# A fused attention and feed-forward kernel on one core: earlier cast, fourth tile partly interleaved, W1 pieces regrouped, last tile stored in three pieces

## Chip, cores, metric

One core of a Trainium2 chip. The metric is the device time of one execution in microseconds (us). Each kernel was run 4 to 6 times, on the same chip together with the kernel before. Engines: PE is TensorE, PEld its weight loads, DVE is VectorE, ACT is ScalarE, POOL is GpSimd, SP is SyncE. A bank is one of the kernel's PSUM tiles, in which matmuls are summed; an eviction is the copy out of it by ACT or DVE. The eight heads are handled in two head groups (hg 0 and 1), each with its own part of the transposed softmax, aT, and of W1.

## The reference

```python
B, H, S, Ns, D = 8, 8, 512, 32, 64
# attention of x over a small state, and of the state over x
scores = x @ state.T / 8 ; a  = softmax(scores)  ; xread = a @ state
scores2 = state @ x.T / 8; a2 = softmax(scores2) ; sread = a2 @ x
t = concat([xread, sread], axis=2)      # to tokens x 512
h = t @ w_in                            # 512 -> 2048
out = (h * sigmoid(h)) @ w_out          # 2048 -> 512
```

The kernel never forms xread. For each batch b it makes `W1 = state @ w_in` (per head), and then `h = a @ W1`. "G1" below is that product (two matmuls of 512 columns for each of 16 slices ft of 128 hidden columns), followed by one silu on ACT. "G2" is the product with w_out: four token tiles tt, each summed over the 16 slices, so 64 matmuls a batch. Tokens of sread are a ninth, smaller group at the end.

## The kernel before

The first batches are special. Nothing is resident yet, so batch 0 makes its W1 in pieces between its matmuls. Three token tiles of batch 0 are summed slice by slice; the fourth (tt = 3) is kept back, to give PE work while ACT, DVE and POOL do the softmax of batch 1. I call that stretch, from the scores of batch 1 to its first G1, the handover.

```python
# start of batch 0 (cut)
for u in range(2): copy(nc.vector, <slots of the state>, ps0[...])   # state placement
cast_x(0, nc.vector, 0, 2, 0, 4); cast_x(0, nc.scalar, 2, 2, 0, 4)
...
pe_transpose_x(0, 1, 2, new_h, (nc.vector, nc.scalar))
norm(0, 0); scores(0, 1, 2); exps(0, 1)
norm(0, 1, ((nc.vector, 0, 4),), 2)
w1_cols(0, [(0, 256)], (nc.scalar, nc.scalar))
...
pe_transpose_a(0, 0, nc.vector); pe_transpose_a(0, 1, nc.vector)
g1_half(0, 0); g1_half(1, 0)

# batch 0 (cut)
banks[:] = ["a1", "a2", "a3"]
W0 = {0: (256, 256), 2: (512, 512), 6: (1024, 512), 10: (1536, 512)}
for ft in range(NFT):
    upto(min(ft + LEAD0[ft], ready))                 # G1 and silu up to there
    if ft in W0: w1_cols(0, [W0[ft]], both)          # W1 of batch 0
    if ft in (5, 9, 11): w1_chunks(1, ({5: 0, 9: 1, 11: 2}[ft],), both)   # W1 of batch 1
    ...
    if ft < 14:
        for tt in range(3): G2(0, tt, ft)
...
# handover to batch 1 (cut)
scores(1, 0); scores(1, 1); exps(1, 0); exps(1, 1)
store(0, 2, nc.scalar)
nc.scalar.activation(warm[:], busy[:, 0:1], func=SILU, bias=0.0)   # table load
store(0, 1, nc.vector)
norm(1, 0); norm(1, 1, ((nc.gpsimd, 0, 2), (nc.vector, 2, 2)))
for ft in range(NFT):
    if ft == 5:  w1_chunks(1, (3,), (nc.scalar, nc.scalar))
    if ft == 11: pe_transpose_a(1, 0, nc.scalar); pe_transpose_a(1, 1, nc.vector)
    if ft >= 14: upto(NFT + ft - 12)
    G2(0, 3, ft)

# the last tile: two halves of 256 columns, each evicted by two engines (cut)
def last_half(b, tt, half):
    ...
    for i, eng in enumerate((nc.vector, nc.scalar)):
        copy(eng, o[:, ds(DM // 4 * i, DM // 4)], ps[:, ds(DM // 4 * i, DM // 4)])
    nc.sync.dma_start(out_sread[ds(512, 32), ds(4 * tt, 4), cols], o[:])
```

The softmax here doesn't subtract the row's maximum and nothing guards it: scores larger than these inputs give would overflow.

Of the kernel before, what the change touches and what calls it, by code (L numbers as in the profile page):

```python
# [8 lines left out]
FP32 = mybir.dt.float32  # L9
BF16 = mybir.dt.bfloat16  # L10
# [8 lines left out]
B = 8  # L19
H = 8  # L20
S = 512
NS = 32
D = 64
DM = 512
# [17 lines left out]
def kernel(  # L42
# [141 lines left out]
    make_identity(nc, ident)  # L184
    ones_beside_x(0, nc.gpsimd)
    load_w_in(0, 256)
    load_w_out(0, 2)
    load_w_in(256, 256)
    load_w_out(2, 2)
# [4 lines left out]
    load_w_in(512)  # L194
    load_w_out(4, 4)

    def load_states():
# [44 lines left out]
    def pe_transpose_x(b, hg, nb=2, new=bank, engs=(nc.vector, nc.scalar), only=None):  # L242
# [3 lines left out]
        for u in range(nb) if only is None else only:  # L246
# [8 lines left out]
            copy(engs[u], xT[b][:, ds(m * u, m), ds(2 * hg, 2), :], ps[:])  # L255

    for u in range(2):
        copy(
            nc.vector,
            slots_of(0)[u].rearrange("p g (k n) -> p g k n", n=NS)[:, :, 0:3:2, :],  # L260
            ps0[ds(64 * u, 64)].rearrange("p (g k) m v -> p g k (m v)", g=2),
        )
    cast_x(0, nc.vector, 0, 2, 0, 4)
    cast_x(0, nc.scalar, 2, 2, 0, 4)
    o_tags = ["o0", "o1"]
# [32 lines left out]

    def scores(b, hg, m=4):
        sc_ps[hg] = []  # L300
        for c in range(4):
            if c % m == 0:
                sc_ps[hg].append(bank([128, m, 4, NS], FP32, "ps_sc"))
            for j in range(2):
                nc.tensor.matmul(
                    sc_ps[hg][-1][:, c % m, ds(2 * j, 2), :],
                    xT[b][:, c, 2 * hg + j, :],
                    stT[:, b, 2 * hg + j, :, :],
                    start=True,
                    stop=True,  # L310
                    skip_group_check=True,
                )
# [81 lines left out]

    def pe_transpose_a(b, hg, eng, other=None):
        ps = bank([128, 4, 128], BF16, "ps_at")
        for c in range(4):
            nc.tensor.transpose(ps[:, c, :], an[b, hg][:, c, :, :], ident[:])  # L398
        if other is None:
            copy(eng, aT[b][:, hg, :, :], ps[:])  # L400
        else:
            copy(eng, aT[b][:, hg, 0:2, :], ps[:, 0:2])
            copy(other, aT[b][:, hg, 2:4, :], ps[:, 2:4])

# [49 lines left out]

    def w1_mms(b, cols):
        pss = {}
        if b not in W1:
            W1[b] = wpool.tile([128, 2, DF], BF16, tag="W1", name="W1")
        for f, n in cols:
            for hg in range(2):  # L460
                pss[f, hg] = bank([128, 512], FP32, "ps_w1")
            for s in range(4):
# [13 lines left out]

    def w1_out(b, cols, engs, pss):
        for f, n in cols:
            for hg in range(2):
                copy(engs[hg], W1[b][:, hg, ds(f, n)], pss[f, hg][:, 0:n])  # L480

    def w1_cols(b, cols, engs):
        w1_out(b, cols, engs, w1_mms(b, cols))

# [9 lines left out]

    def g1_half(k, hg):
        b, ft = divmod(k, NFT)
        if hg == 0:
            h_ps[k] = psH.tile([128, 512], FP32, tag="h1", name="h1")
        nc.tensor.matmul(  # L499
            h_ps[k][:],  # L500
            W1[b][:, hg, ds(128 * ft, 128)],
            aT[b][:, hg, :, :],
            start=(hg == 0),
            stop=(hg == 1),
            skip_group_check=True,
        )

    def emit_G1(k):
        b, ft = divmod(k, NFT)
        if b < B:  # L510
            if k not in h_ps:
                g1_half(k, 0)
            g1_half(k, 1)
            ps = h_ps.pop(k)
# [18 lines left out]
    def G2(b, tt, ft):  # L533
        if ft == 0:
            if b == 0 and tt == 2:
                outs[tt] = psA.tile([128, DM], FP32, tag="a0", name="o_a")
            else:
                i = (tt + (b > 0)) % 2 if tt < 3 else 0
                outs[tt] = psO.tile([128, DM], FP32, tag=f"o{i}", name="o")
# [17 lines left out]

    def last_half(b, tt, half):
        cols = ds(DM // 2 * half, DM // 2)
        ps = bank([128, DM], FP32, "o_half")  # L560
        for ft in range(NFT):
            nc.tensor.matmul(  # L562
                ps[:, 0 : DM // 2],
                gt[b * NFT + ft][:, ds(128 * tt, 128)],
                w_out_sb[:, ft, cols],
                start=(ft == 0),
                stop=(ft == NFT - 1),
                skip_group_check=True,
            )
        o = opool.tile([128, DM // 2], FP32, tag="o_half", name="o_half")  # L570
        for i, eng in enumerate((nc.vector, nc.scalar)):
            copy(eng, o[:, ds(DM // 4 * i, DM // 4)], ps[:, ds(DM // 4 * i, DM // 4)])
        nc.sync.dma_start(out_sread[ds(512, 32), ds(4 * tt, 4), cols], o[:])


    both = (nc.vector, nc.scalar)
    done = [0]
# [10 lines left out]
    keep_busy(1, psH, "h1")  # L588
    pe_transpose_x(0, 1, 2, new_h, (nc.vector, nc.scalar))
    norm(0, 0)  # L590
    scores(0, 1, 2)
    exps(0, 1)
    norm(0, 1, ((nc.vector, 0, 4),), 2)
    w1_cols(0, [(0, 256)], (nc.scalar, nc.scalar))
    nc.scalar.activation(warm[:], busy[:, 0:1], func=SILU, bias=0.0)
    load_w_in(1024)
    load_w_out(8, 4)
# [5 lines left out]
    load_x(2)  # L603
    for i in (1, 2):
        ones_beside_x(i, nc.gpsimd)
    keep_busy(4, psO, "o0")
    pe_transpose_a(0, 0, nc.vector)
    keep_busy(1, psO, "o0")
    pe_transpose_a(0, 1, nc.vector)
    g1_half(0, 0)  # L610
    g1_half(1, 0)



    banks[:] = ["a1", "a2", "a3"]
    turn[0] = 0
    W0 = {0: (256, 256), 2: (512, 512), 6: (1024, 512), 10: (1536, 512)}
    LEAD0 = [2, 2, 2, 2, 2, 3, 2, 3, 3, 2, 2, 3, 3, 3, 2, 1]
    ready = 2
    for ft in range(NFT):  # L620
# [6 lines left out]
        if ft == 13:  # L627
            for hg in range(2):
                cast_x(1, nc.vector, 0, 4, 4 * hg, 4)
            load_x(3)  # L630
        if ft in (5, 9, 11):
            w1_chunks(1, ({5: 0, 9: 1, 11: 2}[ft],), both)
        if ft == 14:
# [3 lines left out]
        if ft < 14:  # L637
            for tt in range(3):
                G2(0, tt, ft)
    for tt in (0, 2, 1):  # L640
        G2(0, tt, 14)
        G2(0, tt, 15)
        if tt == 0:
            store(0, 0, nc.vector)
    at = turn[0] % 3
    banks[:] = banks[at:] + banks[:at] + ["a0"]
    turn[0] = 0
    scores(1, 0)
    scores(1, 1)
    exps(1, 0)  # L650
# [4 lines left out]
    norm(1, 0)  # L655
    norm(1, 1, ((nc.gpsimd, 0, 2), (nc.vector, 2, 2)))
    for ft in range(NFT):
        if ft == 5:
            w1_chunks(1, (3,), (nc.scalar, nc.scalar))
        if ft == 11:  # L660
            pe_transpose_a(1, 0, nc.scalar)
            pe_transpose_a(1, 1, nc.vector)
            for i in (2, 3):
                for c in range(4):
                    cast_x(i, nc.gpsimd, c, 1)
            transpose_x(2)
        if ft >= 14:
            upto(NFT + ft - 12)
        G2(0, 3, ft)
    upto(NFT + 4)  # L670
    store(0, 3, nc.vector)

    for b in range(1, B):
# [3 lines left out]
        for tt in range(4):  # L677
            for ft in range(NFT):
# [24 lines left out]
                if m + 1 < B:  # L703
# [5 lines left out]
                    if at == (2, 10):  # L709
                        transpose_x(m + 1)  # L710
                if n < B and at == (1, 4):
                    if m < B:
# [29 lines left out]
    store(B, 0, nc.scalar)  # L742
    last_half(B, 1, 0)
    last_half(B, 1, 1)
# [28 lines left out]
```

## Time and profile before

| | before |
|---|---|
| median of 4 runs (lowest to highest) | 217.93 us (217.91 to 218.23) |
| span of the profiled run | 216.2 us |
| PE busy | 209.5 us (97%) |
| first silu of batch 0 starts | 12.31 us |
| scores of batch 1 start | 33.78 us |
| first G1 of batch 1 starts | 38.81 us |
| last eviction starts | 212.29 us |

From the page of before: the span, the busy time of each engine (share, number of instructions), and the shares of the chain that ended last.

```profile
span 216.2 us, 3870 instructions
...
PE 209.5 (97%) x1565; PEld 96.6 (45%) x1565; DVE 75.6 (35%) x166; ACT 140.7 (65%) x246; POOL 39.2 (18%) x61
...
PE 90%; DVE 5%; ACT 1%; issue 1%; POOL 0%; POOLq 0%
```

The kernel is PE bound: the chain of waits is a row of matmuls for 90% of the span. The Trainium skill, "Perfetto Trace Analysis", "Identifying the Most-Contended Engine", says that the busy share of matmuls is no good measure of how close a kernel is to its limit, because pipelined instructions look smaller in the trace. Here they look larger: a matmul of 512 columns is drawn 0.38 us long, while back-to-back ones start every 0.216 us. So I count starts.

The timeline of before around one W1 piece (start us, duration us, engine, line, operation, operands, number merged).

```profile
14.67 0.59 PE L499 MATMUL h<-aT,W 128*128 128x512 bf16 x2
...
15.19 0.41 PE L466 MATMUL ps_w<-w_in_sb,stT 64*32 64x512 bf16 x8
...
15.54 0.60 PE L540 MATMUL o<-w_out_sb,g 128*128 128x512 bf16 x2
```

The two G1 matmuls occupy the stream until 14.67 + 2 x 0.216 = 15.10; the next full-size one starts at 15.54. The W1 piece costs 0.44 us. Its eight matmuls (a tile of 64 x 32 each) are worth about one slot of 0.216. I put the rest, 0.22 us, down to entering and leaving the smaller tile size.

The chain names PE nearly throughout. What ACT does at the same time, and PE's last matmuls before G1, from the timeline of before:

```profile
35.18 0.60 ACT L156 ACTIVATE o_sb<-o_a 128x512 f32<-128x512 f32 x1
...
35.81 1.28 ACT L653 ACT_TABLE_LOAD   x1
...
37.21 1.06 ACT L156 ACTIVATE W<-ps_w 128x512 bf16<-128x512 f32 x2
...
38.06 0.81 PE L540 MATMUL o<-w_out_sb,g 128*128 128x512 bf16 x3
38.16 0.60 ACT L156 ACTIVATE aT<-ps_at 128x512 bf16<-128x512 bf16 x1
...
38.81 1.02 PE L499 MATMUL h<-aT,W 128*128 128x512 bf16 x4
```

ACT finishes aT at 38.16 + 0.60 = 38.76, and G1 (which reads aT) starts at 38.81; PE's matmuls before it end their slots at 38.06 + 3 x 0.216 = 38.71. Nor is PE at work all the time that it is drawn busy: by the code, the second bank of the W1 piece is the one that ACT's copy of 35.18 evicts; that copy ends at 35.78, and the second part of the piece starts at 35.84. The piece is drawn 0.83 us long.

The end of before, from the timeline:

```profile
212.29 0.29 DVE L158 COPY o_half<-o_half 128x128 f32<-128x128 f32 x1 [1.46 <-PE o_half L562]
212.62 0.28 ACT L156 ACTIVATE o_half<-o_half 128x128 f32<-128x128 f32 x1 [1.47 <-DVE o_half L158]
```

Two copies in series (the second waits for the first), then the last store of 128 KB; the span ends 3.91 us after the first of them starts.

### The profile page before, as it was taken

To read this page: it belongs to the slowest core of one execution; us is meant where nothing else is said; L and a number is where in the kernel's file an instruction comes from. 1 tells how busy PE (TensorE), PEld (TensorE's weight loads), DVE (VectorE), ACT (ScalarE), POOL (GpSimd) and SP (SyncE) were. 2 spreads that over 40 slices of the span, in tenths; PEclk is the share of its full clock that TensorE was granted. 3 is DMA by queue.
4 is the path that set the end of the run, shared out by engine and by line. 5 is a ranking of instruction groups with operands and counts; after the bars stand their busy time and mean duration, and the time that the engine had idled before them with its cause. 6 is when DMAs were issued, how large, how long until landed. Compare 5 with 4: busy or idle time off the path is not lost.

```text
span 216.2 us, 3870 instructions
## 1 busy us (share of the span) xinstructions
PE 209.5 (97%) x1565; PEld 96.6 (45%) x1565; DVE 75.6 (35%) x166; ACT 140.7 (65%) x246; POOL 39.2 (18%) x61
## 2 busy tenths in 40 slices
PE   7899999999999999999999999999999999999992
PEld 2433344545344444444444444444444444466562
DVE  3733248354961156106610551135312406100010
ACT  3766578799566975699459956886675367644411
POOL 8582013801520042004110402000200000000000
PEclk9999999999999999999999999999999999999999
DMA  6999999693349848373647293114310211011112
GB/s 208 186 201 206 227 340 322 186 277 111 62 98 251 193 106 196 72 222 99 158 92 240 69 186 98 49 52 103 97 49 31 75 49 52 2 49 49 52 50 95
DMA packets 41714, 28.40 MB, mean 131 GB/s; under 512 B 26464, under 2 KB 36576, under 8 KB 41696
## 3 DMA queue, kind: packets, MB, share of 16 engines
q1 hardware_dynamic: 35664, 20.45, 35.5%
q0 software_dynamic: 5888, 7.64, 17.2%
q8 instruction: 12, 0.20, 0.4%
q10 hardware_dynamic: 144, 0.07, 0.1%
q14 instruction: 6, 0.05, 0.1%
HBM read 17.43 MB, written 8.91 MB: 122 GB/s over the span
## 4 chain that ended last, share of the span: by engine, by line
PE 90%; DVE 5%; ACT 1%; issue 1%; POOL 0%; POOLq 0%
PE o L540 49%; PE h L499 26%; PE ps_w L466 4%; PE h L518 3%; PE ps_busy L164 2%; PE o_half L562 2%; DVE W L158 2%; PE o_a L540 1%; DVE rs L378 1%; PE ps_sr L418 1%; DVE rc L434 1%; PE ps_xt L250 1%; PE ps_scT L331 1%; PE ps_at L398 1%; ACT L319 1%
## 5 line engine op out<-in xcount | busy, mean ns | idle before, releaser
L540 PE MATMUL o<-w_out_sb,g 128*128 128x512 bf16 x512 | 136.5, 379 | 0.0
L531 ACT ACTIVATE g<-h 128x512 bf16<-128x512 f32 (+1 forms) x145 | 82.1, 570 | 36.9 <-PE h L499 22.8
L499 PE MATMUL h<-aT,W 128*128 128x512 bf16 x256 | 75.6, 379 | 0.2
L540 PEld LDWEIGHTS <-g 128*128 128x128 bf16 x528 | 49.8, 98 | 57.6 <-issue 3.7
L158 DVE COPY o_sb<-o 128x512 f32<-128x512 f32 x17 | 11.7, 691 | 91.9 <-PE o L540 91.9
L499 PEld LDWEIGHTS <-W 128*128 128x128 bf16 x256 | 24.8, 98 | 31.7 <-DVE W L158 1.6
L158 DVE CAST W<-ps_w 128x512 bf16<-128x512 f32 (+1 forms) x31 | 20.5, 678 | 27.1 <-PE ps_w L466 27.1
L156 ACT ACTIVATE W<-ps_w 128x512 bf16<-128x512 f32 (+1 forms) x35 | 18.7, 574 | 12.1 <-PE ps_w L466 12.0
L158 POOL CAST x_nat<-x_f 128x512 bf16<-128x512 f32 x24 | 14.1, 628 | 33.2 <-DMA x_f<-in_x_dram 22.4
L156 ACT ACTIVATE o_sb<-o 128x512 f32<-128x512 f32 x15 | 8.9, 596 | 12.6 <-PE o L540 9.5
L361 POOL TENSOR_TENSOR an<-e,rcn 128x512 bf16<-128x512 bf16 x5 | 7.6, 1516 | 49.5 <-DVE rcn L359 49.5
L466 PE MATMUL ps_w<-w_in_sb,stT 64*32 64x512 bf16 (+1 forms) x264 | 12.0, 375 | 0.4 <-DVE W L158 0.2
L518 PE MATMUL h<-xmT,w_in_sb 128*128 128x256 bf16 x64 | 9.6, 273 | 0.0
L518 PEld LDWEIGHTS <-w_in_sb 128*128 128x128 bf16 x64 | 6.3, 98 | 3.9
L164 PE MATMUL ps_busy<-busy 128*128 128x512 bf16 x16 | 6.4, 519 | 1.2 <-DVE warm L171 1.2
L466 PEld LDWEIGHTS <-stT 64*32 64x32 bf16 x264 | 3.6, 89 | 8.3 <-issue 6.8
L381 POOL TENSOR_TENSOR an<-exp_nat,rc 128x512 bf16<-128x512 bf16 (+1 forms) x4 | 3.9, 981 | 17.1 <-DVE rc L379 17.1
L718 ACT ACT_TABLE_LOAD x5 | 6.4, 1283 | 0.1
L345 ACT ACTIVATE eT<-ps_scT 128x512 bf16<-128x512 f32 x10 | 5.4, 598 | 1.6 <-PE ps_scT L331 1.6
L358 DVE TENSOR_REDUCE rs<-e 128x32 f32<-128x1024 bf16 x5 | 6.1, 1211 | 0.4 <-DMA e<-eT 0.4
L108 POOL DMA_DIRECT2D x_f<-in_x_dram x4 | 3.3, 849 | 14.3 <-DVE x_rows L158 12.3
L540 PE MATMUL o_a<-w_out_sb,g 128*128 128x512 bf16 x16 | 5.9, 379 | 0.0
(71 smaller groups left out, 102.4 us busy)
## 6 DMA issues: line engine op xcount, KB each, us to landing
out_dram<-o_sb SPq DMA_DIRECT2D x33, 256.0 KB, 2.3
x_f<-in_x_dram SPq DMA_DIRECT2D x4, 1024.0 KB, 6.0
x_f<-in_x_dram POOLq DMA_DIRECT2D x2, 1024.0 KB, 12.0
w_in_sb<-in_moe_w_in_dram POOLq DMA_DIRECT2D x3, 512.0 KB, 9.6
w_out_sb<-in_moe_w_out_dram POOLq DMA_DIRECT2D x3, 512.0 KB, 11.3
x_f<-in_x_dram SPq DMA_DIRECT2D x2, 512.0 KB, 4.5
x_f<-in_x_dram POOLq DMA_DIRECT2D x2, 512.0 KB, 16.1
w_in_sb<-in_moe_w_in_dram POOLq DMA_DIRECT2D x2, 256.0 KB, 7.1
```

Source lines behind the costliest of these rows:

```text
L156: nc.scalar.activation(dst, src, func=COPY, bias=0.0)
L158: eng.tensor_copy(dst, src)
L164: nc.tensor.matmul(ps[:], busy[:, 0:128], busy[:], start=True, stop=True, skip_group_check=True)
L345: nc.scalar.activation(t[:, hg], scT_ps[hg][:], func=EXP, bias=0.0, scale=SCALE)
L358: nc.vector.tensor_reduce(rs[:], e2[b][:], axis=AX, op=ADD)
L361: eng.tensor_tensor(a[:, hg], e2[b][:, hg], rc[:, hg].to_broadcast([128, 4, 4, NS]), op=MULT)
L466: nc.tensor.matmul(pss[f, hg][ds(32 * s, 32), 0:n], stT[ds(r, 64), b, h // 2, s % 2, :], w_in_sb[ds(r, 64), h // 2, ds(f, n)], start=True, ...
L499: nc.tensor.matmul(h_ps[k][:], W1[b][:, hg, ds(128 * ft, 128)], aT[b][:, hg, :, :], start=(hg == 0), stop=(hg == 1), skip_group_check=True,)
L518: nc.tensor.matmul(ps[:, 0:256], w_in_sb[:, kt, ds(128 * ft, 128)], xmT[:, :, kt].rearrange("p t n b -> p t (n b)"), start=(kt == 0), stop ...
L531: nc.scalar.activation(g[:, ds(i, m)], ps[:, ds(i, m)], func=SILU, bias=0.0)
L540: nc.tensor.matmul(outs[tt][:], gt[b * NFT + ft][:, ds(128 * tt, 128)], w_out_sb[:, ft, :], start=(ft == 0), stop=(ft == NFT - 1), skip_gr ...
L718: nc.scalar.activation(warm[:], busy[:, 0:1], func=SILU, bias=0.0)
```

## The change

The intent: start batch 0 sooner; spend fewer switches of tile size on W1; fill the waits of the first slices with matmuls of the fourth tile; shorten the last eviction and store.

```diff
-    ones_beside_x(0, nc.gpsimd)
-    load_w_in(0, 256)
+    load_w_in(0, 128)
+    load_w_in(128, 384)
     load_w_out(0, 2)
-    load_w_in(256, 256)
 ...
+    cast_x(0, nc.vector, 0, 2, 0, 4)
+    cast_x(0, nc.scalar, 2, 2, 0, 4)
     for u in range(2):
         copy(
-            nc.vector,
+            both[u],
 ...
-    pe_transpose_x(0, 1, 2, new_h, (nc.vector, nc.scalar))
+    pe_transpose_x(0, 1, 2, new_h, (nc.vector, nc.vector))
 ...
-    norm(0, 1, ((nc.vector, 0, 4),), 2)
-    w1_cols(0, [(0, 256)], (nc.scalar, nc.scalar))
+    norm(0, 1, ((nc.vector, 0, 2), (nc.vector, 2, 2)))
+    pss0 = w1_mms(0, [(0, 128)])
     nc.scalar.activation(warm[:], busy[:, 0:1], func=SILU, bias=0.0)
+    w1_out(0, [(0, 128)], (nc.scalar, nc.scalar), pss0)
 ...                                     # W1 128..511 before the first G1; aT of hg 0 on ACT,
 ...                                     # of hg 1 on DVE in two parts; G1(0) takes hg 1 first
-    banks[:] = ["a1", "a2", "a3"]
-    W0 = {0: (256, 256), 2: (512, 512), 6: (1024, 512), 10: (1536, 512)}
+    banks[:] = ["a2", "a3"]
+    W0 = {2: (512, 512), 6: (1024, 512), 10: (1536, 512)}
+    F3 = 3
 ...
-        if ft in (5, 9, 11):
-            w1_chunks(1, ({5: 0, 9: 1, 11: 2}[ft],), both)
+        if ft in (5, 9):
+            w1_chunks(1, ({5: 0, 9: 1}[ft],), both)
 ...
-            for tt in range(3):
+            for tt in range(4 if ft < F3 else 3):
                 G2(0, tt, ft)
 ...
-    norm(1, 1, ((nc.gpsimd, 0, 2), (nc.vector, 2, 2)))
-    for ft in range(NFT):
-        if ft == 5:
-            w1_chunks(1, (3,), (nc.scalar, nc.scalar))
-        if ft == 11:
-            pe_transpose_a(1, 0, nc.scalar)
-            pe_transpose_a(1, 1, nc.vector)
+    norm(1, 1, ((nc.vector, 0, 4),))
 ...                                     # the banks (tail_bank) of the merged piece
+    for ft in range(F3, NFT):
+        if ft == 8:
+            w1_cols(1, [(1024, 512), (1536, 512)], both, tail_bank)
+        if ft == 12:
+            pe_transpose_a(1, 0, nc.scalar, new_h)
+        if ft == 13:
+            pe_transpose_a(1, 1, nc.vector, new_h)
-        if ft >= 14:
-            upto(NFT + ft - 12)
+        if ft == 15:
+            upto(NFT + 2)
         G2(0, 3, ft)
-    upto(NFT + 4)
+    upto(NFT + 3)
 ...
-                if n < B and at == (1, 4):
+                if n < B and at == (1, 6 if b == 1 else 4):
 ...
-    last_half(B, 1, 0)
-    last_half(B, 1, 1)
+    last_cols(B, 1, 0, 256, nc.scalar, nc.sync)
+    last_cols(B, 1, 256, 128, nc.vector, nc.scalar)
+    last_cols(B, 1, 384, 128, nc.vector, nc.sync)
```

More of the change, by code (lines that the diff above doesn't have):

```diff
@@ L195 @@
     load_w_out(4, 4)
+    both = (nc.vector, nc.scalar)
     def load_states():
@@ L262 @@
         )
-    cast_x(0, nc.vector, 0, 2, 0, 4)
-    cast_x(0, nc.scalar, 2, 2, 0, 4)
     o_tags = ["o0", "o1"]
@@ L297, with scores @@
     sc_ps = {}
-    def scores(b, hg, m=4):
+    def scores(b, hg, m=4, new=bank):
         sc_ps[hg] = []
@@ L302, in scores @@
             if c % m == 0:
-                sc_ps[hg].append(bank([128, m, 4, NS], FP32, "ps_sc"))
+                sc_ps[hg].append(new([128, m, 4, NS], FP32, "ps_sc"))
             for j in range(2):
@@ L393, in transpose_a, with pe_transpose_a @@
         )
-    def pe_transpose_a(b, hg, eng, other=None):
-        ps = bank([128, 4, 128], BF16, "ps_at")
-        for c in range(4):
-            nc.tensor.transpose(ps[:, c, :], an[b, hg][:, c, :, :], ident[:])
-        if other is None:
-            copy(eng, aT[b][:, hg, :, :], ps[:])
-        else:
-            copy(eng, aT[b][:, hg, 0:2, :], ps[:, 0:2])
-            copy(other, aT[b][:, hg, 2:4, :], ps[:, 2:4])
+    def pe_transpose_a(b, hg, eng, new=bank, c0=0, n=4):
+        ps = new([128, n, 128], BF16, "ps_at")
+        for c in range(n):
+            nc.tensor.transpose(ps[:, c, :], an[b, hg][:, c0 + c, :, :], ident[:])
+        copy(eng, aT[b][:, hg, ds(c0, n), :], ps[:])
     xm_ps = {}
@@ L453, in place_xm, with w1_mms @@
                 )
-    def w1_mms(b, cols):
+    def w1_mms(b, cols, new=bank):
         pss = {}
@@ L460, in w1_mms @@
             for hg in range(2):
-                pss[f, hg] = bank([128, 512], FP32, "ps_w1")
+                pss[f, hg] = new([128, 512], FP32, "ps_w1")
             for s in range(4):
@@ L475, in w1_mms, with w1_out, w1_cols @@
         return pss
-    def w1_out(b, cols, engs, pss):
+    def w1_out(b, cols, engs, pss, at=0):
         for f, n in cols:
             for hg in range(2):
-                copy(engs[hg], W1[b][:, hg, ds(f, n)], pss[f, hg][:, 0:n])
-    def w1_cols(b, cols, engs):
-        w1_out(b, cols, engs, w1_mms(b, cols))
+                copy(engs[hg], W1[b][:, hg, ds(f + at, n)], pss[f, hg][:, ds(at, n)])
+    def w1_cols(b, cols, engs, new=bank):
+        w1_out(b, cols, engs, w1_mms(b, cols, new))
     def w1_chunks(b, fbs, engs):
@@ L493, with g1_half @@
     h_ps = {}
-    def g1_half(k, hg):
+    def g1_half(k, hg, first=0):
         b, ft = divmod(k, NFT)
-        if hg == 0:
+        if hg == first:
             h_ps[k] = psH.tile([128, 512], FP32, tag="h1", name="h1")
@@ L502, in g1_half @@
             aT[b][:, hg, :, :],
-            start=(hg == 0),
-            stop=(hg == 1),
+            start=(hg == first),
+            stop=(hg != first),
             skip_group_check=True,
@@ L510, in emit_G1 @@
         if b < B:
-            if k not in h_ps:
+            if k == 0:
+                g1_half(k, 1, 1)
+                g1_half(k, 0, 1)
+            else:
                 g1_half(k, 0)
-            g1_half(k, 1)
+                g1_half(k, 1)
             ps = h_ps.pop(k)
@@ L534, in G2 @@
         if ft == 0:
-            if b == 0 and tt == 2:
-                outs[tt] = psA.tile([128, DM], FP32, tag="a0", name="o_a")
+            if b == 0 and tt >= 2:
+                outs[tt] = psA.tile([128, DM], FP32, tag=f"a{tt - 2}", name="o_a")
             else:
@@ L555, in store, with last_cols @@
             nc.sync.dma_start(out_sread[ds(512, 32), ds(4 * tt, 4), :], o[:])
-    def last_half(b, tt, half):
-        cols = ds(DM // 2 * half, DM // 2)
-        ps = bank([128, DM], FP32, "o_half")
+    def last_cols(b, tt, f, n, eng, queue):
+        cols = ds(f, n)
+        ps = bank([128, DM], FP32, "o_part")
         for ft in range(NFT):
             nc.tensor.matmul(
-                ps[:, 0 : DM // 2],
+                ps[:, 0:n],
                 gt[b * NFT + ft][:, ds(128 * tt, 128)],
@@ L569, in last_half @@
             )
-        o = opool.tile([128, DM // 2], FP32, tag="o_half", name="o_half")
-        for i, eng in enumerate((nc.vector, nc.scalar)):
-            copy(eng, o[:, ds(DM // 4 * i, DM // 4)], ps[:, ds(DM // 4 * i, DM // 4)])
-        nc.sync.dma_start(out_sread[ds(512, 32), ds(4 * tt, 4), cols], o[:])
-    both = (nc.vector, nc.scalar)
+        o = opool.tile([128, n], FP32, tag=f"o_part{f}", name="o_part")
+        copy(eng, o[:], ps[:, 0:n])
+        queue.dma_start(out_sread[ds(512, 32), ds(4 * tt, 4), cols], o[:])
     done = [0]
@@ L603 @@
     load_x(2)
-    for i in (1, 2):
+    for i in range(3):
         ones_beside_x(i, nc.gpsimd)
-    keep_busy(4, psO, "o0")
-    pe_transpose_a(0, 0, nc.vector)
-    keep_busy(1, psO, "o0")
-    pe_transpose_a(0, 1, nc.vector)
-    g1_half(0, 0)
-    g1_half(1, 0)
-    banks[:] = ["a1", "a2", "a3"]
+    keep_busy(3, psH, "h1")
+    pss0 = w1_mms(0, [(128, 384)])
+    keep_busy(2, psH, "h1")
+    new_o = lambda sh, dt, nm: psO.tile(sh, dt, tag=o_tags.pop(), name=nm)
+    o_tags[:] = ["o0", "o1"]
+    pe_transpose_a(0, 0, nc.scalar, new_o)
+    pe_transpose_a(0, 1, nc.vector, new_o, 0, 2)
+    pe_transpose_a(0, 1, nc.vector, bank, 2, 2)
+    upto(1)
+    w1_out(0, [(128, 128)], (nc.vector, nc.vector), pss0)
+    w1_out(0, [(128, 256)], both, pss0, 128)
+    banks[:] = ["a2", "a3"]
     turn[0] = 0
-    W0 = {0: (256, 256), 2: (512, 512), 6: (1024, 512), 10: (1536, 512)}
+    W0 = {2: (512, 512), 6: (1024, 512), 10: (1536, 512)}
     LEAD0 = [2, 2, 2, 2, 2, 3, 2, 3, 3, 2, 2, 3, 3, 3, 2, 1]
-    ready = 2
+    F3 = 3
+    ready = 4
     for ft in range(NFT):
@@ L644 @@
             store(0, 0, nc.vector)
-    at = turn[0] % 3
-    banks[:] = banks[at:] + banks[:at] + ["a0"]
+    banks[:] = ["a2", "a3", "a0", "a1"]
     turn[0] = 0
-    scores(1, 0)
-    scores(1, 1)
+    scores(1, 0, new=new_h)
+    scores(1, 1, new=new_h)
     exps(1, 0)
@@ L655, with tail_bank @@
     norm(1, 0)
-    norm(1, 1, ((nc.gpsimd, 0, 2), (nc.vector, 2, 2)))
-    for ft in range(NFT):
-        if ft == 5:
-            w1_chunks(1, (3,), (nc.scalar, nc.scalar))
-        if ft == 11:
-            pe_transpose_a(1, 0, nc.scalar)
-            pe_transpose_a(1, 1, nc.vector)
+    norm(1, 1, ((nc.vector, 0, 4),))
+    tail_tags = ["a2", "a3", "a0", "o0"]
+    def tail_bank(shape, dtype, name):
+        tag = tail_tags.pop(0)
+        return (psO if tag == "o0" else psA).tile(shape, dtype, tag=tag, name=name)
+    for ft in range(F3, NFT):
[5 more added lines that the diff above has]
+            pe_transpose_a(1, 1, nc.vector, new_h)
             for i in (2, 3):
```

## The prediction

> **What bounds the kernel.** The page shows PE busy 97% of a 216.2 us span at full granted clock, and the chain of waits is 90% PE. From 77 us on the chain is back-to-back matmuls (22.62 us per batch, one 512-column matmul every 0.216 us); the change leaves these batches alone. What can move is the ramp to about 41 us, and the end. In the timeline the first G1 matmul of batch 0 starts at 11.35 us and the first of batch 1 at 38.81. The matmuls, transposes and scores between them are worth about 23.5 us at the issue rate, so about 4 us are lost there.
>
> The losses, from the timeline: each separate W1 piece costs 0.44 us in the stream where its 8 packed matmuls are worth 0.22, so 0.22 us goes at each entry and exit. The Trainium skill, "TensorEngine Tiling (Array Packing)", Key Properties, says that changing the tiling mode drains the engine; the trace agrees (PEld of the W1 matmuls idles up to 0.42 us beforehand). Further, 0.22 us is lost three times while G1 waits for a fresh W1 eviction, about 0.6 us in the piece at 35.4, about 0.4 around 12.2 to 14.
>
> **Terms (estimates from these durations).**
>
> 1. Start. The DVE cast of x moves from 5.38 to about 4.9. I expect at most 0.1 us of that at the first silu of batch 0 (12.31 before): both hg1 copies are now on DVE, so its chain (copies 0.42 each, reduce 0.68, reciprocal 0.25) and the POOL multiply (1.05, ends 10.39) end at about the same time, and aT of hg0 is copied on ACT behind a 1.28 us table load.
> 2. W1 columns 256 to 511 leave the loop (0.22 switch + 0.11 work), and the fourth tile's first three matmuls (0.65) fill waits around 13 to 16.5. The following G1 still starts 0.2 to 0.3 later by the clock, having done more. Net gain about 0.4.
> 3. Two rotating banks instead of three: the W1 piece at 20.7 waits for evictions of the piece before it. Loss 0.1 to 0.2.
> 4. The piece at ft 11 goes: gain 0.44 before the scores of batch 1 (33.78). Its work returns in the merged piece, so one switch (0.22) is really removed.
> 5. Batch 0 to 1 handover. The latency chain from scores to aT (5.0 us) stays: exp, table load, reduce, POOL multiply. But DVE now multiplies all of hg1 (0.7 to 0.9) and evicts two W1 parts (1.3) before aT (0.42), with three fewer matmuls as filler. I expect G1 of batch 1 about 0.4 us later relative to the scores, with one matmul less remaining: loss 0.2 to 0.35.
> 6. Later W1 of batch 2: around nothing. The non-PE chain from 49.6 to 58.9 ends that stage anyway.
> 7. End: 212.29 to 212.90 are a DVE and an ACT copy in series (0.29, 0.28) before the last store (2.1 to landing). One copy now, half the bytes: gain 0.3 to 0.4.
>
> Sum: 0.1+0.4-0.15+0.44-0.3+0.35, about 0.85 us. **Predicted 217.1 us, 216.2 to 217.9 eight times in ten; faster by over 2%: 0.01, within 2%: 0.98, slower: 0.01.**
>
> **Signs.** First silu at 12.2 to 12.3; scores of batch 1 at 33.0 to 33.3; first G1 of batch 1 at 38.3 to 38.7 with a PE gap just before it ended by DVE's aT copy; unchanged 22.6 us per batch; last store issued about 0.3 us sooner after the last matmul.
>
> **What would make it wrong.** x of batch 1 is waited for at 30.5 us (cast waits for the DMA): with DMA busy throughout, an earlier PE may find data late, and gain less. The handover stall could be much smaller (then 216.5) or swallow everything. A later first silu would cancel term 2.

## More of the kernel before

The handover of before, from the chain of waits (start us, length us, what):

```profile
33.94 0.47 PE ps_sc L305 x16
34.41 1.08 PE o L540 x5
35.49 0.32 PE ps_w L466
35.81 0.03 issue
35.84 0.41 PE ps_w L466 x7
36.25 1.40 PE o L540 x6
37.65 0.57 PE ps_at L398 x8
38.22 0.65 PE o L540 x3
38.87 0.97 PE h L499 x4
```

## The result, and the profile after

| | before | after |
|---|---|---|
| median of 4 runs | 217.93 us | 217.59 us (217.32 to 217.71) |
| ratio, 95% interval | | 0.9979 (0.9962 to 0.9997) |
| span of the profiled run | 216.2 | 215.9 |
| mean granted clock of it | 1.000 | 0.998 |
| first silu of batch 0 | 12.31 | 12.62 |
| scores of batch 1 | 33.78 | 33.98 |
| first G1 of batch 1 | 38.81 | 39.01 |
| last eviction starts | 212.29 | 212.62 |

A ratio is the mean time of one kernel's fast runs over that of the other's of the same rounds, so not quite the ratio of the medians. The time lies inside the predicted range, but the gain is 0.34 us by medians (0.46 by the ratio), about half of the 0.85 us that I had forecast; a repeat, after_again below, gives 0.61 by medians and 0.48 by the ratio. In this trace not one of the signs for the ramp came true: the first silu, the scores and the first G1 of batch 1 are all later than before, not earlier. (In the trace of the repeat the first silu, 12.21, and the first G1, 38.60, lie where I said; the scores, 33.56, do not.)

From the page of after, the lines that answer to those of before:

```profile
span 215.9 us, 3875 instructions
...
PE 207.1 (96%) x1555; PEld 97.4 (45%) x1581; DVE 76.6 (35%) x169; ACT 140.0 (65%) x245; POOL 38.8 (18%) x60
...
PE 88%; DVE 6%; ACT 3%; issue 1%
```

ACT's share of the chain rose from 1% to 3%. The chain of waits of after, in the handover, shows where:

```profile
34.14 0.25 PE ps_sc L306 x8
34.39 0.02 issue
34.41 1.08 ACT exp_nat L320 x2
35.50 0.49 ACT o_sb L156
35.99 0.02 issue
36.01 1.28 ACT L658
37.29 0.01 issue
37.30 0.20 ACT warm L658
37.50 0.97 ACT W L156 x2
38.47 0.50 ACT aT L156
38.97 0.04 issue
39.01 1.13 PE h L496 x4
```

Where before had a row of matmuls, there is now a row of ACT instructions: two exps, an eviction, a table load, the evictions of W1, the copy of aT. The handover still lasts 5.03 us (33.98 to 39.01; before 33.78 to 38.81), with 12 matmuls of the fourth tile in it instead of 14 (of the three moved, the third came off the work behind the first G1) and 16 packed W1 matmuls instead of 8. The busy times of PE in that stretch, from the view of time windows (before, then after; the columns are window, length, and busy us with counts of PE, PEld, DVE, ACT, POOL, then the clock, the share of DMA and GB/s):

```profile
34.25:38.81 4.56, 4.53 (x36) 1.93 (x33) 3.24 (x7) 4.48 (x8) 2.84 (x4) 1.00 0.99 352
```

```profile
34.45:39.01 4.56, 4.03 (x41) 1.64 (x39) 4.34 (x9) 4.48 (x8) 2.84 (x4) 1.00 0.99 352
```

ACT is busy for 4.48 of the 4.56 us in both kernels. PE was busy for 4.53 and is now for 4.03. One matmul of after has no record here (its weight load, at 37.45, has one); it closes the gap of 0.15 us before the second transposes, so that about 4.2 is the better figure. The other 0.37 us are PE's wait for aT just before G1: the work that the change took out of this stretch became idle time. DVE is now nearly as full, 4.34 us, and its copy of aT, of head group 1, comes last:

```profile
38.88 0.41 DVE L158 COPY aT<-ps_at 128x512 bf16<-128x512 bf16 x1
```

It ends at 39.29, behind the start of G1. The second matmul of G1, which reads it, starts at 39.34, 0.33 us after the first instead of 0.22: another 0.11 us, outside the handover as I measure it.

The end of after, from the timeline:

```profile
211.73 0.29 DVE L158 COPY o_part<-o_part 128x128 f32<-128x128 f32 x1 [5.40 <-PE o_part L562]
...
212.62 0.29 DVE L158 COPY o_part<-o_part 128x128 f32<-128x128 f32 x1 [0.60 <-PE o_part L562]
```

One copy, then a store of 64 KB; the span ends 3.28 us after it starts, 0.63 us sooner than before by that measure (spans are given to 0.1 us, so by 0.05 more or less).

### The profile page after: what moved, and what is told of

Read it like the earlier page. It is cut to its first block, busy times and chain, and to the rows that moved or that the text cites. A ratio compares the mean times of both kernels' runs of the same rounds, so it can differ in the third digit from the quotient of the medians.

```text
span 215.9 us, 3875 instructions
## 1 busy us (share of the span) xinstructions
PE 207.1 (96%) x1555; PEld 97.4 (45%) x1581; DVE 76.6 (35%) x169; ACT 140.0 (65%) x245; POOL 38.8 (18%) x60
## 4 chain that ended last, share of the span: by engine, by line
PE 88%; DVE 6%; ACT 3%; issue 1%
PE o L540 47%; PE h L496 25%; PE ps_w L463 3%; PE h L518 3%; PE ps_busy L164 2%; PE o_a L540 2%; PE o_part L562 2%; DVE W L158 2%; DVE rs L379 1%; PE ps_xt L251 1%; DVE an L382 1%; PE ps_sr L415 1%; DVE rc L431 1%; ACT exp_nat L320 1%; PE ps_scT L332 1%
## 5 line engine op out<-in xcount | busy, mean ns | idle before, releaser
L540 PE MATMUL o<-w_out_sb,g 128*128 128x512 bf16 x483 | 129.3, 379 | 1.9 <-issue 1.1
L496 PE MATMUL h<-aT,W 128*128 128x512 bf16 x245 | 73.0, 379 | 0.9 <-DVE aT L158 0.4
L158 DVE COPY o_sb<-o 128x512 f32<-128x512 f32 x16 | 11.0, 690 | 90.1 <-PE o L540 90.1
L158 DVE CAST W<-ps_w 128x512 bf16<-128x512 f32 (+2 forms) x34 | 21.5, 653 | 25.8 <-PE ps_w L463 25.8
L156 ACT ACTIVATE W<-ps_w 128x512 bf16<-128x512 f32 (+2 forms) x34 | 17.9, 566 | 12.6 <-PE ps_w L463 12.6
L463 PE MATMUL ps_w<-w_in_sb,stT 64*32 64x512 bf16 (+2 forms) x264 | 11.3, 375 | 0.7 <-DVE W L158 0.7
L540 PE MATMUL o_a<-w_out_sb,g 128*128 128x512 bf16 x31 | 9.8, 379 | 0.1
L382 POOL TENSOR_TENSOR an<-exp_nat,rc 128x512 bf16<-128x512 bf16 x3 | 3.1, 1046 | 17.9 <-ACT eT L346 11.4
```

Source lines behind the costliest of these rows:

```text
L156: nc.scalar.activation(dst, src, func=COPY, bias=0.0)
L158: eng.tensor_copy(dst, src)
L463: nc.tensor.matmul(pss[f, hg][ds(32 * s, 32), 0:n], stT[ds(r, 64), b, h // 2, s % 2, :], w_in_sb[ds(r, 64), h // 2, ds(f, n)], start=True, ...
L496: nc.tensor.matmul(h_ps[k][:], W1[b][:, hg, ds(128 * ft, 128)], aT[b][:, hg, :, :], start=(hg == first), stop=(hg != first), skip_group_ch ...
L540: nc.tensor.matmul(outs[tt][:], gt[b * NFT + ft][:, ds(128 * tt, 128)], w_out_sb[:, ft, :], start=(ft == 0), stop=(ft == NFT - 1), skip_gr ...
```

## The experiments

Two theories stood at the beginning. One: the change does what I predicted, but the start of the runs hides it, because TensorE warms up at different moments. Two: the gains before the scores of batch 1 are real but the handover swallows them. The table of marks, read from the timeline of each kernel's profiled run, is the main instrument: once the first silu has started, the rest of an execution repeats to a few hundredths, while whole times of one kernel scatter by 0.3 to 1 us (before by 1.55). (From silu to last eviction after and after_again differ by 0.01 us; before and before_end, whose order of work differs only at the end, by 0.11, of which 0.07 lies before the scores.) There is one trace of each kernel. Columns: start of the first silu; from there to the scores of batch 1; from these to the first G1 of batch 1; from it to the start of the last eviction; first silu to last eviction; last eviction to the end of the span.

| kernel | first silu | to scores | handover | to last eviction | silu to last eviction | end |
|---|---|---|---|---|---|---|
| before | 12.31 | 21.47 | 5.03 | 173.48 | 199.98 | 3.91 |
| before_end | 12.04 | 21.54 | 5.04 | 173.51 | 200.09 | 3.37 |
| after | 12.62 | 21.36 | 5.03 | 173.61 | 200.00 | 3.28 |
| after_again | 12.21 | 21.35 | 5.04 | 173.62 | 200.01 | 3.28 |
| after_hg0first | 12.47 | 21.36 | 5.03 | 173.62 | 200.01 | 3.32 |
| after_wlate | 12.69 | 21.36 | 4.50 | 173.56 | 199.42 | 3.29 |
| after_F0 | 12.23 | 21.12 | 5.03 | 173.63 | 199.78 | 3.29 |
| wlate_F0 | 12.33 | 21.10 | 4.81 | 173.67 | 199.58 | 3.29 |
| after_nomerge | 12.48 | 21.81 | 4.54 | 173.51 | 199.86 | 3.36 |
| wlate_hg0 | 12.11 | 21.48 | 4.50 | 173.56 | 199.54 | 3.35 |
| after_end2 | 12.28 | 21.35 | 5.03 | 173.58 | 199.96 | 3.66 |
| after_xtboth | 12.56 | 21.36 | 5.03 | 173.62 | 200.01 | 3.33 |
| F0_3banks | 12.35 | 21.02 | 5.04 | 173.62 | 199.68 | 3.27 |
| wlate_hg0_dve | 11.99 | 21.51 | 4.49 | 173.54 | 199.54 | 3.37 |

Every kernel gave the right result, and every ratio is within 1% of 1.

### after_again: the kernel after, once more

No edit.

> The kernel after, unchanged, once more. Theory A (the TensorE clock): the trace of after shows 8 transposes of x at 5.5 us taking 1.06 us against 0.62 before, so its matmuls were still cold until about 6.9 us; its four runs fall into 217.3 to 217.5 (clock 1.0) and 217.7 (0.997). If that is only the phase of warming up, runs scatter between 217.3 and 217.7 again, and a profile at clock 1.0 shows the first silu about 0.2 to 0.3 us earlier than 12.62. Theory B (work order alone): the first silu stays at 12.6 whatever the clock.

Measured: median 217.31 us over five runs (217.29 to 217.78), before on the same chip 217.92 over eleven (217.65 to 218.25); ratio 0.9978 (0.9966 to 0.9990). From the timeline, the first transposes of x and the first silu, in the trace of after and then in this one:

```profile
5.47 1.06 PE L251 MATMUL ps_xt<-ident,x_rows 128*128 128x128 bf16 x8
...
12.62 0.66 ACT L531 ACTIVATE g<-h 128x256 bf16<-128x256 f32 x2 [0.88 <-PE h L496]
```

```profile
5.38 0.62 PE L251 MATMUL ps_xt<-ident,x_rows 128*128 128x128 bf16 x8 [0.25 <-DVE x_rows L158]
...
12.21 0.66 ACT L531 ACTIVATE g<-h 128x256 bf16<-128x256 f32 x2 [0.88 <-PE h L496]
```

The same program; eight transposes take 1.06 us in one execution and 0.62 in the other, and the first silu differs by 0.41 us. Theory A holds. (The mean granted clock does not tell the two states apart: the trace of after_wlate has 1.000 and transposes of 1.06 us. I call a trace warm when these transposes take 0.62 us, and cold when they take 1.06.) It agrees with the Trainium skill, "TensorE: Matmul & The Clock Gate", "Part 1: The HAM clock gate", which says that the warm-up is judged in a window that runs freely of the kernel's start, so that the number of cold matmuls varies from run to run. That explains the scatter of whole times, but not the missing gain: from the first silu to the last eviction this warm run needs 200.01 us, the cold one 200.00, before 199.98. Of all the work on the ramp, nothing is left behind the first silu. Whether the new start itself is earlier or later than the old one is less clear: with transposes of 0.62 us, the old start gives a first silu at 12.31 (before) and 12.04 (before_end), the new one 12.21 here.

### before_end: the new end alone

```diff
 # before, with last_cols of the change in place of last_half
+    last_cols(B, 1, 0, 256, nc.scalar, nc.sync)
+    last_cols(B, 1, 256, 128, nc.vector, nc.scalar)
+    last_cols(B, 1, 384, 128, nc.vector, nc.sync)
```

> Before with the new end alone (256, 128 and 128 columns, one copy each). My prediction: 0.3 to 0.4 us faster than before (217.55). From the two traces (last matmul 0.33 later after the change, yet the span 0.3 shorter): about 0.6 us faster (217.3). If it is 0.6, then everything else in the change adds up to a loss of about 0.2 us.

Measured: median 217.52 us (six runs), ratio 0.9985 (0.9973 to 0.9997), on the same chip as after_again with 217.31 and 0.9978. By the marks, last eviction to end fell from 3.91 to 3.37 us. The whole times alone can't tell 0.35 from 0.6 us, since the interval allows 0.07 to 0.59 (0.0003 and 0.0027 of 217.9); the marks say 0.54. The end is worth more than I gave it, and about as much as the whole change. (The last evictions start 0.03 us later after the first G1, 173.51 against 173.48, so 0.51 is nearer to the net gain.)

### after_hg0first: the first G1 takes head group 0 first

```diff
             if k == 0:
-                g1_half(k, 1, 1)
-                g1_half(k, 0, 1)
+                g1_half(k, 0)
+                g1_half(k, 1)
```

> After with the first G1 of batch 0 accumulating head group 0 first. In the trace of after aT of group 0 is ready at 11.75 and that of group 1 at 11.94, and both halves run after 11.99. If this order costs time: the first silu 0.2 us earlier, the whole 0.1 to 0.2 us faster than after. If the loop behind it is held by other waits: no difference.

Measured: first silu at 12.47 against 12.62 in the trace of after, both with transposes of 1.06 us, so in the same cold state: 0.15 us earlier. Median 217.26 us, ratio 0.9972 (0.9960 to 0.9984); against after_again's 217.31 the gain is not clear of the scatter. The order did cost time at the start: before had done its first head group while waiting for the second, after begins both when the later one is ready.

### after_wlate: evictions of W1 behind aT

```diff
-            w1_cols(1, [(1024, 512), (1536, 512)], both, tail_bank)
+            pss1 = w1_mms(1, [(1024, 512), (1536, 512)], tail_bank)
 ...
             pe_transpose_a(1, 1, nc.vector, new_h)
+            w1_out(1, [(1024, 512), (1536, 512)], both, pss1)
```

> After with the four evictions of the merged W1 piece of batch 1 moved behind the two aT copies on DVE and ACT. If those evictions hold the handover (chain of waits: ACT W 0.97, then aT 0.50, then G1 at 39.01): first G1 of batch 1 0.4 to 0.7 us earlier, the whole 0.3 to 0.5 us faster than after. Rival: the handover is bound by the silus that follow (ACT 0.6 each), then under 0.1.

Measured: the handover falls from 5.03 to 4.50 us and first silu to last eviction from 200.00 to 199.42. Median 217.17 us (216.80 to 217.37), ratio 0.9960 (0.9947 to 0.9972). Its chain of waits:

```profile
34.68 1.08 PE o_a L540 x5
35.76 0.34 PE ps_w L463 x8
36.10 0.01 issue
36.11 0.41 PE ps_w L463 x8
36.52 0.97 PE o_a L540 x4
37.49 0.26 PE ps_at L399 x4
37.75 0.02 issue
37.77 0.60 ACT aT L156
```

The handover is a row of matmuls again until aT. G1 starts at 38.55, as soon as PE is free (38.12 + 2 x 0.216). This shows what held the handover in after: not the amount of work on PE, but the place of the evictions. The edit moved two on ACT and two on DVE. That those on ACT held the first G1 is read from the chain, which runs through ACT's aT; DVE's were not moved alone.

### after_F0 and wlate_F0: no interleaving, with early and with late evictions

```diff
-    F3 = 3
+    F3 = 0
```

and in wlate_F0 the edit of after_wlate as well.

> After with the fourth tile not interleaved (its first three matmuls go back behind the scores of batch 1). My prediction's term 2 counted the interleaving as 0.4 us of gain: then this is 0.3 to 0.5 us slower than after, and first silu to last matmul grows from 200.0 to about 200.4. New theory (the three matmuls were the filler of a handover that lasts 5.03 us from the scores to the first G1 of batch 1 whatever fills it): silu to scores shrinks by 0.3 to 0.5 us (21.36 in after), scores to G1 grows to 5.2 to 5.5, PE bound again, and the sum stays within 0.2 us of after.

> The late evictions of the merged W1 piece, without interleaving. New theory: with all of the filler back, PE and not ACT ends the handover, so moving the evictions gains at most 0.1 us over the kernel without interleaving alone (with interleaving it gained 0.5 to 0.6 from first silu to last matmul), and this is 0.3 to 0.5 us slower than late evictions with interleaving. Rival (late evictions are worth about 0.5 by themselves): as fast as late evictions with interleaving.

Measured, after_F0: median 217.24 us, ratio 0.9967 (0.9953 to 0.9981). First silu to scores 21.12, so the interleaving costs 0.24 us there (21.36); the handover stays at 5.03. My prediction's 0.4 us of gain is refuted: without interleaving the stretch from silu to last eviction is 0.22 us shorter (199.78 against 200.00). But my new expectation was wrong in one point too. I had said that the handover would grow to 5.2 to 5.5 us, PE bound. It did not move: even with all the fourth tile's matmuls behind the scores it is ACT that ends it (aT ready at 38.33, PE free at 38.16, G1 at 38.38).

wlate_F0: median 217.08 us, ratio 0.9961 (0.9946 to 0.9976). The handover is 4.81 us, not 5.03; the late evictions gain 0.20 us from silu to last eviction without interleaving (199.78 to 199.58), and gained 0.58 with it (200.00 to 199.42). I expected at most 0.1 here; the rival expected 0.5. The four kernels together, first silu to last eviction:

| | W1 evicted before aT | after aT |
|---|---|---|
| three matmuls interleaved | 200.00 | 199.42 |
| none interleaved | 199.78 | 199.58 |

Interleaving costs 0.22 us while ACT bounds the handover and gains 0.16 when it doesn't. It was the right idea in front of the wrong handover. These are differences of marks, one trace each; the whole times (217.17 and 217.08 with late evictions, in different calls) do not tell the last two kernels apart.

### after_nomerge: a W1 piece of batch 1 back at ft 11

```diff
-        if ft in (5, 9):
-            w1_chunks(1, ({5: 0, 9: 1}[ft],), both)
+        if ft in (5, 9, 11):
+            w1_chunks(1, ({5: 0, 9: 1, 11: 2}[ft],), both)
 ...
-            w1_cols(1, [(1024, 512), (1536, 512)], both, tail_bank)
+            w1_cols(1, [(1536, 512)], both, tail_bank)
```

> After with columns 1024 to 1535 of W1 of batch 1 back as a piece of their own at ft 11. Prediction's term 4: 0.2 us slower (one more switch). New theory (handover bound by ACT, which now evicts one half of W1 less before aT): silu to scores grows by 0.44 us, scores to G1 shrinks by 0.3 to 0.5 us, sum within 0.15 us of after.

Measured: to the scores 21.81 us, 0.45 more than after; the handover 4.54, 0.49 less; silu to last eviction 199.86, 0.14 less than after. Median 217.47 us, ratio 0.9973 (0.9958 to 0.9988). The price of a separate piece is what I had read from the trace of before (0.44), and merging did save it. But the merged piece brought its evictions in front of aT, and the handover took the whole saving back (0.49). Counted to the last eviction, merging lost 0.14 us.

### after_end2: two pieces at the end instead of three

```diff
-    last_cols(B, 1, 256, 128, nc.vector, nc.scalar)
-    last_cols(B, 1, 384, 128, nc.vector, nc.sync)
+    last_cols(B, 1, 256, 256, nc.vector, nc.sync)
```

> After with the last two pieces of 128 columns joined to one of 256, evicted by DVE alone. From the start of the last copy to the end of the span: before 3.91 us (two copies in series, 128 KB), after 3.29 (one copy of 128 columns, 64 KB). If only the serial second copy mattered (0.28 to 0.33), this comes to 3.4 to 3.5; if the smaller last store matters as much, to about 3.7 to 3.8.

Measured: 3.66 us from the last eviction to the end of the span. Against before (3.91) it lacks only the second copy in series: 0.25 us. Against after (3.28 to 3.29) it has a larger last piece: 0.37 us, of which the copy itself is 0.13 (0.42 us for 256 columns, 0.29 for 128) and the rest belongs to the store of twice the bytes. So the gain at the end has two parts, and I had counted mainly the first. Median 217.68 us, ratio 0.9979 (0.9951 to 1.0007), against a before of 218.13 us.

### after_xtboth: the xT copies on two engines again

```diff
-    pe_transpose_x(0, 1, 2, new_h, (nc.vector, nc.vector))
+    pe_transpose_x(0, 1, 2, new_h, (nc.vector, nc.scalar))
```

> After with the two hg1 copies of xT on DVE and ACT, as before. My prediction put the lost start on both being on DVE. If so: the reduction of head group 0 starts 0.3 us earlier and the first silu 0.1 to 0.3 us earlier at the same state of the clock. Rival: the exps of head group 1 on ACT then come later and its reduction waits for them: first silu no earlier, or up to 0.2 us later.

Measured: the reduction of head group 0 starts at 8.16 us (8.49 in the trace of after), as expected, but that of head group 1 at 9.44 (9.37), where it waits for the exps on ACT, and the first silu comes at 12.56 (12.62). Both runs have the reduced mean clock of 0.998. The rival holds, but for 0.06 us: the chain runs through head group 1, and my reason for the lost start was the wrong one. Median 217.65 us, ratio 0.9974 (0.9949 to 0.9999).

### F0_3banks: three banks in turn

```diff
-    F3 = 3
+    F3 = 0
-            if b == 0 and tt >= 2:
-                outs[tt] = psA.tile([128, DM], FP32, tag=f"a{tt - 2}", name="o_a")
+            if b == 0 and tt == 2:
+                outs[tt] = psA.tile([128, DM], FP32, tag="a0", name="o_a")
-    banks[:] = ["a2", "a3"]
+    banks[:] = ["a1", "a2", "a3"]
-    tail_tags = ["a2", "a3", "a0", "o0"]
+    tail_tags = ["a2", "a3", "a0", "a1"]
```

> No interleaving and three banks in turn (the fourth tile back in its old bank). Against no interleaving with two banks (first silu to scores 21.12): term 3 of the prediction said 0.1 to 0.2 us; expect 20.95 to 21.05. If two banks cost nothing: 21.12.

Measured: 21.02 us from silu to scores against 21.12 with two banks. Two banks cost 0.10 us, as predicted. Median 217.20 us, ratio 0.9956 (0.9932 to 0.9979).

### wlate_hg0 and wlate_hg0_dve: versions meant to beat both

```diff
 # after_wlate and after_hg0first together; in wlate_hg0_dve also
-            w1_out(1, [(1024, 512), (1536, 512)], both, pss1)
+            w1_out(1, [(1024, 512), (1536, 512)], (nc.vector, nc.vector), pss1)
```

> Late evictions and head group 0 first together: the candidate for a better version. If the two gains add (0.15 before the first silu, 0.5 to 0.6 in the handover): median about 216.9, 0.4 to 0.6 us faster than after and about 1.0 us faster than before.

> Late evictions, head group 0 first, and all four late evictions on DVE, so that ACT goes from aT straight to the first silu of batch 1. The chain of waits of the late kernel runs ACT aT, W, W, silu, then the third G1 of batch 1. If that wait matters: third G1 0.1 us earlier and the whole up to 0.1 us faster than late evictions with head group 0 first (216.98); if the next silus hold PE anyway: the same.

Measured: wlate_hg0 216.98 us against 217.93 of before, ratio 0.9961 (0.9943 to 0.9978); wlate_hg0_dve 216.73 against 218.13, ratio 0.9932 (0.9913 to 0.9952). Both are faster than before, and by their marks faster than after. That the second beats the first is not shown: the third G1 of batch 1 starts 1.31 us after the first instead of 1.34 (I had expected 0.1 less), silu to last eviction is 199.54 in both, and the two were not run in one call. The gain of the start is also partly given back. In these two warm traces the stretch to the scores takes 21.48 and 21.51 us, not 21.36: the second cast of x of batch 1 begins at 31.08 and 30.99, after waiting 0.66 and 0.68 us for its load, and the transposes behind it take 1.17 and 1.20 us instead of 1.06. An earlier PE meets data that come no earlier.

## Why the prediction was right or wrong

The time fell inside the range of 216.2 to 217.9 us, but near its upper part, and it did so partly because the errors of terms 2 and 7 have opposite signs. That is luck; and the range, which reached to 0.03 us below the time of before, was wide for a change of this size. The terms, in us of gain, with the marks that measure each:

| term | predicted | measured | how |
|---|---|---|---|
| 1 start | +0.1 | not settled: +0.10 or -0.17 | first silu 12.31 (before) or 12.04 (before_end), and 12.21 (after_again), all warm |
| 2 interleaving and W1 columns 256 to 511 | +0.4 | -0.24 | to scores 21.36 and 21.12 (after_F0); the W1 columns: nothing, see below |
| 3 two banks | -0.1 to -0.2 | -0.10 | 21.12 and 21.02 |
| 4 piece at ft 11 gone | +0.44 | +0.45 | 21.81 and 21.36 |
| 5 handover and ramp of batch 1 | -0.2 to -0.35 | -0.13 | 5.03 and 5.03; 173.48 and 173.61 (0.03 of it belongs to the end: 173.51 in before_end) |
| 6 later W1 of batch 2 | 0 | 0 | below |
| 7 end | +0.3 to 0.4 | +0.63 | 3.91 and 3.28 |
| sum | +0.85 | +0.61 and the start | whole times: 0.34 and, in the repeat, 0.61 by medians; 0.46 and 0.48 by the ratios |

The step that failed is term 2, "the fourth tile's first three matmuls (0.65) fill waits around 13 to 16.5 ... Net gain about 0.4". I carried that 0.4 forward as if the scores of batch 1 came 0.4 us sooner (my sign for them was 33.0 to 33.3). But in the kernel before, the matmuls of the fourth tile stand behind these scores, not in front of them. Work pulled in front of the scores makes the scores later, and it is repaid only if the stretch that it left becomes shorter. The filling itself went as I had said: three matmuls worth 0.65 us were done for a delay of 0.24 (predicted: "0.2 to 0.3 later by the clock"). What failed is that I booked the 0.4 us of work done ahead as a net gain. I counted three matmuls done ahead as time gained, and left it to term 5 to say what the handover would do, where I treated its length as a loss of some tenths. Terms 2 to 4 by the marks give -0.24 - 0.10 + 0.45 = +0.11, which is the whole change from silu to scores (21.47 to 21.36); so by this sum the W1 columns moved out of the loop gave nothing measurable either; no run tests them alone. Term 4 was right in size for its stretch, but it too was booked in full: I had written that only 0.22 of the 0.44 us was really removed, and after_nomerge shows that the handover took back all of it.

The stretch could not become shorter. In every kernel where ACT evicts two halves of W1 in front of aT, the handover is 5.03 or 5.04 us: before, after, with and without interleaving. In before the chain of waits showed only PE, because PE's work and ACT's ended within 0.1 us of each other (PE free at 38.71, ACT's aT ready at 38.76, G1 at 38.81). Term 5 had the mechanism half right: I named a latency chain that stays, and DVE's copy of aT as its end. The copy that holds the first G1 is ACT's; DVE's, as I had said, comes late as well, and holds the second half of that G1 for 0.11 us. That fits most of the 0.13 in the table (not tested alone): the first silu of batch 1 starts 0.74 us after the first G1 instead of 0.63. I also expected the handover to lengthen relative to the scores, and it did not. What it lost is the filler: PE now waits 0.37 us for aT at its end.

Term 1 brought no gain that the traces show, and its sign is not settled. The cast does move forward (transposes at 5.38 in after_again; 5.86 in before and 5.58 in before_end). But the two traces of the old start, 12.31 and 12.04, and the six warm ones of the new start with the order unchanged, 12.21 to 12.48, overlap. In before the transposes of the state, behind which the old start casts x, took 0.42 us; in before_end and after_again they took 0.30. Between these last two the new start is 0.17 later, and the trace shows where: its lead of 0.20 at the transposes is gone at the second reciprocal (9.67 in both), the multiply in two parts takes 0.89 us (0.70 in one), and the first G1 does both halves after the last copy. The order of the two head groups accounts for 0.15 us (after_hg0first); wlate_hg0 and wlate_hg0_dve, warm and with the old order, have their first silu at 12.11 and 11.99. The copies on DVE, which I had named, account for no more than 0.06 (after_xtboth). One wait I had overlooked: in seven of the twelve traces with the new start, the W1 piece of 384 columns waits 0.18 to 0.47 us for its load of w_in, and the transposes of aT stand behind it on PE. In the four warm ones with the order unchanged G1 starts at 11.61 to 11.71, without the wait at 11.58 (after_again) or 11.86 (after_nomerge, whose second transposes of x start 0.27 us later).

Term 6 was right, and shows a wait that moves; no run changes it alone. These are the two waits of the W1 pieces of batch 2, from the timelines of before and after:

```profile
51.90 1.14 PE L466 MATMUL ps_w<-w_in_sb,stT 64*32 64x512 bf16 x16
...
58.94 0.41 PE L466 MATMUL ps_w<-w_in_sb,stT 64*32 64x512 bf16 x8 [0.25 <-DVE W L158]
```

```profile
52.62 0.71 PE L463 MATMUL ps_w<-w_in_sb,stT 64*32 64x512 bf16 x16
...
59.23 0.41 PE L463 MATMUL ps_w<-w_in_sb,stT 64*32 64x512 bf16 x8 [0.68 <-DVE W L158]
```

The first piece stalls 0.43 us less (1.14 to 0.71), and the second waits 0.43 us more (0.25 to 0.68), because a chain of ACT and DVE work ends there. From the scores of batch 2 (49.38 and 49.67) to that point both kernels need 9.56 us.

Term 7 had the right mechanism and about half the size: the series of two copies is 0.25 us of it, the smaller last copy and store 0.37 (after_end2).

Of the signs, these came true: a gap of PE in the handover just before G1 (0.37 us, ended by ACT and not by DVE), batches of 22.6 us, and the last store issued 0.3 us sooner (its copies end 0.61 us after the last eviction starts in before, 0.29 in after). Of what I said could make it wrong, "a later first silu" did happen in the cold trace of after, and late data for batch 1 showed only in the faster versions.

Still open: whether the new start gains or loses anything, since there are two traces of the old one; what DVE's share in the handover is; and whether all evictions on DVE help.

## What to carry to other kernels

Before you move filler out of a stretch, ask whether another engine ends the stretch at the same moment: the chain of waits names one engine, and a tie looks like a single cause. Work done ahead is time gained only where the next latency chain is shorter for it; so shorten that chain first (here four evictions, two of them on ACT, moved behind the copies of aT: 0.58 us), and then the filler pays. When effects are smaller than the scatter of whole times, measure from a mark behind the cause of the scatter to another mark.

## What the Trainium skill lacked or had wrong

- "TensorEngine Tiling (Array Packing)", "Key Properties", says that a change of tiling mode drains TensorE, but gives no price. Here a separate piece of eight 64x32 matmuls costs 0.44 to 0.45 us in the stream, of which about 0.22 are work.
- "TensorE: Matmul & The Clock Gate", Part 1, is right that the warm-up depends on the run (eight transposes 1.06 or 0.62 us in one program), and calls its cost small against a kernel. Here it moved the first silu by 0.41 us (0.2% of the time), about as much as the whole change under study; no page says to compare from a mark behind it.
- "Perfetto Trace Analysis", "Identifying the Most-Contended Engine", looks for one engine. None of its advice covers a tie such as the handover of before, with PE drawn busy for 4.53 and ACT for 4.48 of 4.56 us, where taking work from PE gained nothing. The section also says that pipelined matmuls look smaller in the trace; here they are drawn larger, 0.38 us for a slot of 0.216.
